# The second channel product of the last four groups, by seven block products instead of eight

## The chip, the cores and the metric

The kernel runs on one core of a Trainium2 chip. The core has five engines that each work through their own queue in order: TensorE (PE, matrix products into PSUM), VectorE (DVE) and ScalarE (ACT) for elementwise work, GpSimd (POOL) and SyncE (SP); DMA transfers are issued from the queues of SP, ACT and POOL. The metric is the device time of one execution in microseconds; lower is better.

## The reference, cut to what matters

The input is 2048 tokens of 512 channels. A state-space convolution along the tokens comes first, then a mixer block, each under layer norms and modulations. What matters here is the tail of the mixer:

```python
x1 = x + hs                                   # hs: shifted mixing product @ w2
h2 = _gelu(_layernorm(x1, axis=-1) @ w3) @ w4 # w3: 512 x 1376, w4: 1376 x 512
return x1 + h2
...
x = x + gb * _B_ref(h, B_w1, B_w2, B_w3, B_w4)
```

All is float32. The kernel multiplies in the reduced format fp32r and keeps the precision by splitting each operand into a high part (the value rounded to fp32r) and a low part (the rest): a product a·b is computed as ah·bh + ah·bl + al·bh, three matmuls in place of one.

## The kernel before

The first 360 us or so compute the convolution and the first mixing steps. The end, from `chan(0)` on, is eight groups of 256 tokens (two tiles of 128 tokens; block `b = 2g + i` of the residual `X2`). The order of instructions on every engine is written out by hand: inside the manual schedule each engine executes its instructions in program order.

A group has its 256 normalised tokens transposed in `hl` (high and low parts, four tiles of 128 channels each). Then, on TensorE:

- `first(f2)` (`chan_first`, L953): 256 columns of `w3` (two chunks of 128, `f = 2 f2` and `2 f2 + 1`), 24 matmuls that stream 256 tokens each, into one of two PSUM buffers `pm`. ScalarE evaluates gelu twice from that buffer, once rounded (`gh`) and once in float32 (`gf`); VectorE forms `gl = gf - gh` (L964). `f2 = 5` is only 96 columns.
- `second(f2)` (`chan_second`, L982 with L972, L973, L980): for both token tiles `i` the products of `gh` and `gl` with rows of `w4`, streaming 512 output columns each, summed over all 11 chunks in two PSUM banks `pa0`, `pa1`: 22 matmuls for each of the three lines in a group, 66 in all.
- the next group's part: `chan_w2` (L918), the mixing product `hs` of the next group, 24 matmuls of 512 columns into two PSUM buffers `ph`; the residual is added by VectorE (L916), then statistics (L779, L780; `rstd` on GpSimd, L774 and L775), `chan_norm` (L938), `chan_add` (L944, L945) and eight transposes (L812) whose high and low parts (`parts_of`, L815) are the next group's `hl`.

A group runs first(0), first(1), second(0), first(2), second(1), and so on, so that each `second` lies one `first` behind the `first` that feeds it. At its end `chan_out` (L988) multiplies both sums by the modulation `mods[5]`, adds them to `X2` (L991, L992) and issues the output DMAs (L995). Groups 1 to 3 also carry the first mixing product (`mix_half`, with `w1`) of a later group; groups 4 to 7 don't. Group 7 has no next group, and its last `second` calls are reordered so that the sums of tile 0 end before those of tile 1.

PSUM has eight banks, all in use here: two for transposes (`pT`), two `pm`, two `ph`, `pa0` and `pa1`.

Of the kernel before, what the change touches and what calls it, by code (L numbers as in the profile page):

```python
# [7 lines left out]
F32 = mybir.dt.float32  # L8
F32R = mybir.dt.float32r
# [104 lines left out]
def body(ctx, tc, A):  # L114
# [697 lines left out]
                    T.transpose(ps[j][:, k % 2, i * 128:i * 128 + 128], x[:, i, k * 128:k * 128 + 128], ident)  # L812
        return ps

    def parts_of(ps):  # L815
        hi = [cm.tile([128, 2, 256], F32R, name=f"nh{j}") for j in range(2)]
        lo = [cm.tile([128, 2, 256], F32R, name=f"nl{j}") for j in range(2)]
        for j in range(2):
            act(hi[j], ps[j])
            V.tensor_sub(lo[j], ps[j], hi[j].bitcast(F32))  # L820
        return [hi[k // 2][:, k % 2] for k in range(4)], [lo[k // 2][:, k % 2] for k in range(4)]
# [23 lines left out]
    def mix_norm(g):  # L845
        h, mv, r, nm = mh[g]
        for i in range(2):
            act(h[:, i], h[:, i], AF.Identity, scale=r[:, i:i + 1], bias=nm[:, i:i + 1])

    def three(p, wh, wl, hl, c):  # L850
        hi, lo = hl
        for k in range(4):
            T.matmul(p, wh[:, k, c], hi[k], start=(k == 0), stop=False)  # L853
            T.matmul(p, wl[:, k, c], hi[k], start=False, stop=False)  # L854
        for k in range(4):
            T.matmul(p, wh[:, k, c], lo[k], start=False, stop=(k == 3))  # L856
# [40 lines left out]
        V.tensor_sub(w, w.bitcast(F32), wh.bitcast(F32))  # L897
        win[g] = wh, w

    def chan_mod(g, i):  # L900
        if i == 0:
            cn[g] = cm.tile([128, 2, 512], F32, name="h2")
        modulate(cn[g][:, i], 2 * g + i)

    def chan_sum(g, i):
        wh, wl = win[g]
        p = psm.tile([128, 512], F32, name="ph")
        s = slice(i * 128, i * 128 + 128)
        for f in range(4):
            T.matmul(p, wh[:, f, s], W2h[:, f], start=(f == 0), stop=False)  # L910
            T.matmul(p, wh[:, f, s], W2l[:, f], start=False, stop=False)  # L911
        for f in range(4):
            T.matmul(p, wl[:, f, s], W2h[:, f], start=False, stop=(f == 3))  # L913
        if i == 1:
            del win[g]
        return lambda: V.tensor_add(cn[g][:, i], cn[g][:, i], p)  # L916
# [13 lines left out]
        rstd(r, mv[:, :, 1])  # L930
        cs[g] = mv, r

    def chan_norm(g):
        h = cn[g]
        mv, r = cs.pop(g)
        n = cm.tile([128, 2, 512], F32, name="h2")
        for i in range(2):
            V.tensor_scalar(n[:, i], h[:, i], mv[:, i, 0:1], r[:, i:i + 1], op0=OP.subtract, op1=OP.mult)  # L938
        return n
# [10 lines left out]
        act(go, p, AF.Gelu_apprx_tanh)  # L950
        mix_out(t, hf, go)

    def chan_first(hl, f2):  # L953
# [5 lines left out]
        gf = c2p.tile([128, 2, 256], F32, name="gf")  # L959
# [4 lines left out]
        V.tensor_sub(gl[:m, :ne], gf[:m, :ne], gh[:m, :ne].bitcast(F32))  # L964
        return gh, gl, ne, m

    def second_high(acc, part, f2, i):
        gh, gl, ne, m = part
        s = slice(i * 128, i * 128 + 128)
        for e in range(ne):  # L970
            f = f2 * 2 + e
            T.matmul(acc[i], gh[:m, e, s], W4h[:m, f], start=(f == 0), stop=False)  # L972
            T.matmul(acc[i], gh[:m, e, s], W4l[:m, f], start=False, stop=False)  # L973

    def second_low(acc, part, f2, i):
# [9 lines left out]
        for i in range(2):  # L985
            second_low(acc, part, f2, i)

    def chan_out(g, acc, i, qs):  # L988
        b = 2 * g + i
        o = c2p.tile([128, 512], F32, name="gf")  # L990
        V.tensor_mul(o, acc[i], mods[5])  # L991
        V.tensor_add(X2[:, b], X2[:, b], o)  # L992
        n = 128 // len(qs)
        for k, q in enumerate(qs):
            q.dma_start(A["out"][b, k * n:k * n + n], X2[k * n:k * n + n, b])  # L995

    def chan(g, hl):
        t = g + 3 if 0 < g < 4 else None
        nx = g + 1 if g < 7 else None
        acc = [psm.tile([128, 512], F32, name=f"pa{i}", bufs=1) for i in range(2)]  # L1000
        part, st = {}, {}

        def first(f2):
            part[f2] = chan_first(hl, f2)

        def second(f2):
            chan_second(acc, part.pop(f2), f2)

        def mod(i):
            if t is not None:  # L1010
                if i == 0:
                    mix_mod1(t)
                    mix_mod2(t, 0)
                else:
                    mix_mod2(t, 1)
                    mix_norm(t)

        def turn():
            if t is not None:
                st["hl"] = parts_of(transposed(mh.pop(t)[0]))  # L1020

        def half(hf):
            if t is not None:
                mix_half(t, st["hl"], hf)
                if t < 6:
                    first_stat(2 * t + 2 + hf)

        def nxt(f, *a):
            if nx is not None:
                return f(nx, *a)  # L1030

        if g == 0:
            first(0)
# [25 lines left out]
        else:  # L1059
            first(0)  # L1060
            mod(0)
            first(1)
            mod(1)
            second(0)
            nxt(chan_split)
            first(2)
            nxt(chan_mod, 0)
            second(1)
            turn()
            nxt(chan_mod, 1)  # L1070
            first(3)
            half(0)
            second(2)
            nxt(chan_w2)
            nxt(chan_stats)
            first(4)
            n = nxt(chan_norm)
            nxt(chan_add)
            half(1)
            second(3)  # L1080
            first(5)
            r = parts_of(transposed(n)) if nx is not None else None
            if g < 7:
                second(4)
            if g < 6:
                chan_load(g + 2)
            if g < 7:
                second(5)
            else:
                second_high(acc, part[4], 4, 0)  # L1090
                second_high(acc, part[4], 4, 1)
                for i in range(2):
                    second_low(acc, part[4], 4, i)
                    second_high(acc, part[5], 5, i)
                    second_low(acc, part[5], 5, i)
        for i in range(2):
            chan_out(g, acc, i, (Y,) if g < 7 else (Y, S))
        return r

    splits = []  # L1100

# [13 lines left out]
    with tc.manual_schedule():  # L1115
# [190 lines left out]
        first_stats(4)  # L1306
        chan_load(1)
        for g in range(8):
            r = chan(g, r)


# [16 lines left out]
```

## Time and profile before

| what | value |
|---|---|
| time, median of 3 runs | 678.95 us (677.28 to 679.72) |
| time of the profiled execution | 677.66 us |
| its span, first to last instruction | 675.9 us |
| mean granted TensorE clock | 0.997 |
| TensorE busy, share of the span | 94% |
| VectorE, ScalarE, GpSimd busy | 73%, 50%, 17% |
| group 3 | 487.50 to 530.72 us, 43.22 us |
| groups 4, 5, 6 | 36.56 us each, from 530.72 us to 640.40 us |
| group 7 | from 640.40 us, last matmul at about 670.6 us |

Rows of the profile name an engine, a source line, the tile written and the tiles read, the shape, a count, and times in microseconds (means in ns). PE is the matmul, PEld the loading of the stationary operand ahead of it. The chain of waits lists the work that ended last, in order of time: a start, the time counted for it, and the instruction. A matmul is recorded with its whole latency, so neighbours overlap; in the chain each is counted only with what it adds.

### The profile page before, as it was taken

The numbers are of one execution on the slowest core, as the hardware profiler recorded it, in microseconds if no ns is written. First come the engines' busy times: TensorE is split into PE (matmuls) and PEld (weight loads), VectorE is DVE, ScalarE is ACT, GpSimd is POOL, SyncE is SP. The second block draws the span as 40 slices with busy tenths as digits, with TensorE's granted clock in tenths as the row PEclk, the third lists the DMA queues.
The fourth block names the chain that finished last, engine by engine and source line by source line (L and its number), as shares of the span: only waits on it lengthen the run. The fifth ranks groups of instructions, "written<-read, shape, count | busy, mean of one in ns | idle before, by whom it ended". The sixth has DMA issues, their size and how long they took to land.

```text
span 675.9 us, 16884 instructions
## 1 busy us (share of the span) xinstructions
PE 636.7 (94%) x7205; PEld 508.2 (75%) x7205; DVE 494.2 (73%) x797; ACT 335.8 (50%) x511; POOL 113.7 (17%) x220
## 2 busy tenths in 40 slices
PE   2899999999999998988999999999999999999996
PEld 1556555665568876645889899898998989898895
DVE  7889999999996897897889777454674445363622
ACT  5778998898884666624456334132141213122121
POOL 2102212112207133203643002010010000000000
PEclk9999999999999999998999999999999999999999
DMA  9602274642838999966386020110100201010001
GB/s 318 277 2 75 75 230 107 197 136 76 294 71 296 302 361 377 366 199 194 118 267 232 1 64 1 55 40 16 57 22 31 64 18 46 1 63 1 1 32 31
DMA packets 49923, 86.43 MB, mean 128 GB/s; under 512 B 4532, under 2 KB 38328, under 8 KB 47256
## 3 DMA queue, kind: packets, MB, share of 16 engines
q1 hardware_dynamic: 44904, 60.97, 28.3%
q0 software_dynamic: 4624, 23.86, 9.8%
q8 instruction: 56, 0.92, 0.6%
q10 hardware_dynamic: 320, 0.52, 0.3%
q14 instruction: 19, 0.16, 0.1%
HBM read 59.12 MB, written 32.90 MB: 136 GB/s over the span
## 4 chain that ended last, share of the span: by engine, by line
PE 72%; DMA 5%; DVE 5%; ACT 3%; issue 2%; POOL 1%; SPq 1%; ACTq 0%; DVEq 0%; POOLq 0%
PE xx L440 7%; PE pm L856 7%; PE pm L854 7%; PE pm L853 7%; PE pa L972 6%; PE pa L973 6%; PE pa L980 6%; PE pk L673 4%; PE kp L490 3%; DMA w4l<-Dw 2%; PE pz L695 2%; PE pk L643 2%; PE ph L911 2%; PE ph L910 2%; PE ph L913 2%
## 5 line engine op out<-in xcount | busy, mean ns | idle before, releaser
L122 ACT ACTIVATE gh<-pm 128x512 fp32r<-128x512 f32 (+1 forms) x48 | 26.9, 561 | 199.2 <-PE pm L856 199.2
L853 PE MATMUL pm<-nh,w3h 128*128 128x256 f32 (+1 forms) x352 | 85.9, 278 | 0.0
L854 PE MATMUL pm<-nh,w3l 128*128 128x256 f32 (+1 forms) x352 | 85.7, 279 | 0.1
L964 DVE TENSOR_TENSOR gl<-gf,gh 128x512 fp32r<-128x512 f32 (+1 forms) x48 | 30.9, 643 | 68.1 <-ACT gf L122 68.1
L972 PE MATMUL pa<-w4h,gh 128*128 128x512 f32 (+1 forms) x176 | 69.6, 395 | 0.0
L973 PE MATMUL pa<-w4l,gh 128*128 128x512 f32 (+1 forms) x176 | 68.9, 392 | 0.0
L854 PEld LDWEIGHTS pm<-nh,w3l 128*128 128x128 f32 (+1 forms) x352 | 65.2, 185 | 2.0 <-DVE w3l L767 0.3
L853 PEld LDWEIGHTS pm<-nh,w3h 128*128 128x128 f32 (+1 forms) x352 | 65.3, 186 | 1.4
L856 PE MATMUL pm<-nl,w3h 128*128 128x256 f32 (+1 forms) x352 | 54.9, 277 | 0.1
L774 POOL TENSOR_TENSOR rs<-mv,eps_t 128x1 f32<-128x1 f32 (+1 forms) x35 | 9.2, 264 | 267.3 <-DVE mv L780 251.5
L980 PE MATMUL pa<-w4h,gl 128*128 128x512 f32 (+1 forms) x176 | 48.0, 390 | 0.0
L441 PE MATMUL xx<-MG,ON 64*128 64x512 f32 x160 | 47.1, 390 | 0.0
L440 PE MATMUL xx<-MG,ON 64*128 64x512 f32 x160 | 47.1, 390 | 0.0
L856 PEld LDWEIGHTS pm<-nl,w3h 128*128 128x128 f32 (+1 forms) x352 | 46.6, 185 | 0.3 <-DVE nl L820 0.3
L916 DVE TENSOR_TENSOR h<-h,ph 128x512 f32<-128x512 f32 x16 | 11.0, 688 | 45.0 <-PE ph L913 45.0
L458 DVE SCALAR_TENSOR_TENSOR e<-tr,p 128x512 f32<-128x512 f32 x64 | 41.1, 684 | 1.7 <-ACT tr L122 1.4
L467 DVE TENSOR_TENSOR e<-tr,p 128x1024 f32<-128x1024 f32 x32 | 39.0, 1218 | 1.1 <-ACT tr L122 1.1
L490 PEld LDWEIGHTS kp<-e,e 128*32 128x32 f32 x2048 | 30.1, 110 | 12.7 <-issue 7.5
L468 DVE TENSOR_TENSOR e<-tr,m 128x1024 f32<-128x1024 f32 x32 | 39.0, 1218 | 0.0
L122 ACT ACTIVATE p<-xx 128x1024 f32<-128x1024 f32 (+1 forms) x40 | 37.5, 980 | 2.1 <-PE xx L258 0.6
L980 PEld LDWEIGHTS pa<-w4h,gl 128*128 128x128 f32 (+1 forms) x176 | 33.0, 188 | 7.1
L673 PE MATMUL pk<-VK,xu 64*64 64x128 f32 x768 | 35.9, 270 | 2.2 <-issue 2.2
(259 smaller groups left out, 1709.8 us busy)
## 6 DMA issues: line engine op xcount, KB each, us to landing
VU<-vs SPq DMA_DIRECT2D x64, 128.0 KB, 3.6
ld<-VU SPq DMA_DIRECT2D x16, 512.0 KB, 7.5
ZT<-z POOLq DMA_DIRECT2D x30, 256.0 KB, 6.3
Dw<-in_w POOLq DMA_DIRECT2D x8, 688.0 KB, 4.6
xu<-in_u SPq DMA_DIRECT2D x4, 1024.0 KB, 8.6
KX<-in_x POOLq DMA_DIRECT2D x4, 1024.0 KB, 9.0
ld<-ZT SPq DMA_DIRECT2D x8, 512.0 KB, 5.6
win<-GD SPq DMA_DIRECT2D x32, 128.0 KB, 2.5
```

What stands on the lines that cost most here:

```text
L122: return S.activation(out, in_, f, bias=bias, scale=scale)
L440: T.matmul(x[:, :512], la, ma, start=(i == 0), stop=(i == len(ops) - 1))
L441: T.matmul(x[:, 512:], lb, mb, start=(i == 0), stop=(i == len(ops) - 1))
L458: V.scalar_tensor_tensor(e0[:, 1, a], tr[:, 1, 0], 1.0 - 2.0 * a, mg[:, a], op0=OP.mult, op1=OP.mult)
L490: T.matmul(kp[32 * j:32 * j + 32, (k % 2) * 4 + g], e1[:, r, d], e0[:, r, :, d * 32:d * 32 + 32], start=(r == 0), stop=(r == 1), skip_grou ...
L673: T.matmul(p[gh][kk * 64:kk * 64 + 64, i, ro], w, VK[jh][rows, ri * 32 + k1].rearrange("p j g -> p (j g)"), start=(ri == 0), stop=(ri == 1 ...
L853: T.matmul(p, wh[:, k, c], hi[k], start=(k == 0), stop=False)
L854: T.matmul(p, wl[:, k, c], hi[k], start=False, stop=False)
L856: T.matmul(p, wh[:, k, c], lo[k], start=False, stop=(k == 3))
L972: T.matmul(acc[i], gh[:m, e, s], W4h[:m, f], start=(f == 0), stop=False)
L973: T.matmul(acc[i], gh[:m, e, s], W4l[:m, f], start=False, stop=False)
L980: T.matmul(acc[i], gl[:m, e, s], W4h[:m, f], start=False, stop=(f == 10))
```

## The change

For groups 4 to 7 `chan` is replaced by `chan_late`. There, two neighbouring chunks of the hidden columns (a pair `p`, chunks 2p and 2p+1), the two token tiles and the two halves of the 512 output columns are taken as a 2 x 2 by 2 x 2 block product, and computed with seven block products (Winograd's form of Strassen's scheme) instead of eight. A block product is 128 x 128 x 256.

- `pair_load`, `pair_sums`, `pair_split`: for each of five pairs, four blocks of `w4` (128 x 256) are loaded by DMA into rows of `X2` that are no longer needed, combined in place by four subtractions on VectorE, and split into high parts (ScalarE) and low parts (VectorE). Pairs 0 to 2 are made in group 3, pairs 3 and 4 in group 4. They live where `W1h`, `W1l`, spare tiles and unused halves of `W4h`, `W4l` are.
- `fast_first` replaces `chan_first` for five pairs (four in group 7): gelu once over 512 columns to `xa` and once over 384 to `ha`; four sums of 128 columns on VectorE (`xs`), their high part `hs` on ScalarE, then the low parts `la` (384) and `ls` (512) on VectorE.
- `fast_second` replaces `chan_second` for a pair: 21 matmuls that stream 256 columns, into eight half banks `R[0]` to `R[7]` (`pa0`, `pa1` and both `ph`).
- `fast_rest`: chunk 10 (96 rows), 12 matmuls of 256 columns.
- `fast_sum` replaces `chan_out`: VectorE combines the eight half banks (a copy and six sums of 256, one of 512), and then multiplies and adds to `X2` as before. In group 7 it comes between first(4) and first(5), with a copy and five sums, and chunks 8 to 10 go the old way into the transposes' banks.
- `chan_w2_late`: the next group's mixing product uses the `pm` buffers, since both `ph` are taken.

```diff
+    def pair_sums(p):
+        x = praw[p]
+        V.tensor_sub(x[0], x[1], x[0])
+        V.tensor_sub(x[1], x[3], x[1])
+        V.tensor_sub(x[3], x[3], x[0])
+        V.tensor_sub(x[2], x[2], x[3])
...
+    def fast_first(hl, f2):
...
+        act(fl(xa), pf, AF.Gelu_apprx_tanh)
+        act(fl(ha)[:, 128:], pf[:, 128:], AF.Gelu_apprx_tanh)
+        V.tensor_add(xs[:, 0], xa[:, 0], xa[:, 2])
+        V.tensor_sub(xs[:, 2], xa[:, 1], xa[:, 0])
+        V.tensor_sub(xs[:, 1], xs[:, 0], xa[:, 1])
+        V.tensor_sub(xs[:, 3], xa[:, 3], xs[:, 1])
+        act(hs, xs)
+        V.tensor_sub(fl(la)[:, 128:], fl(xa)[:, 128:], fl(ha)[:, 128:].bitcast(F32))
+        V.tensor_sub(ls, xs, hs.bitcast(F32))
...
+    def fast_second(R, part, p):
...
+        turns = ((0, ha[:, 1], la[:, 1], bh["11"], bl["11"]), (1, ha[:, 3], la[:, 3], bh["21"], bl["21"]),
+                 (4, ha[:, 2], la[:, 2], th[2], tl[2]), (5, hs[:, 3], ls[:, 3], bh["22"], bl["22"]),
+                 (2, hs[:, 2], ls[:, 2], th[1], tl[1]), (3, hs[:, 0], ls[:, 0], th[0], tl[0]),
+                 (6, hs[:, 1], ls[:, 1], th[3], tl[3]))
+        for r, x, _, wh, wl in turns:
+            T.matmul(R[r], x, wh, start=(p == 0 and r in (0, 4, 2, 6)), stop=False, skip_group_check=True)
+            T.matmul(R[r], x, wl, start=False, stop=False, skip_group_check=True)
+        for r, _, x, wh, wl in turns:
+            T.matmul(R[r], x, wh, start=False, stop=False, skip_group_check=True)
...
+    def fast_sum(g, banks, R, rest=True):
+        o = row2(4)
+        q = o.rearrange("p i (h c) -> p (i h) c", h=2)
...
+        V.tensor_copy(q[:, 1], R[0])
+        V.tensor_add(q[:, 2], q[:, 1], R[1])
+        V.tensor_add(q[:, 1], q[:, 1], R[6])
+        for j in range(2):
+            V.tensor_add(q[:, 3 * j], q[:, 1], R[2 + j])
+        V.tensor_add(q[:, 1], q[:, 0], R[3])
+        if rest:
+            V.tensor_add(q[:, 1], q[:, 1], R[7])
+        V.tensor_add(q[:, 0::3], q[:, 0::3], v(banks[2]))
+        for i in range(2):
+            b = 2 * g + i
+            V.tensor_mul(o[:, i], o[:, i], mods[5])
+            V.tensor_add(X2[:, b], X2[:, b], o[:, i])
...
     def chan(g, hl):
...
+            if g == 3:
+                pair_sums(0)
             half(1)
             second(3)
+            if g == 3:
+                pair_split(0, blocks(W1h)[:4], blocks(W1h)[4:])
+                pair_sums(1)
+                pair_sums(2)
             first(5)
...
+            if g == 3:
+                pair_split(1, blocks(W1l)[:4], blocks(W1l)[4:])
+            second(4)
+            chan_load(g + 2)
+            if g == 3:
...
+                pair_split(2, blocks(t4[0]) + blocks(t4[1]), blocks(t4[2]) + blocks(t4[3]))
+                pair_load(3, 4)
+            second(5)
...
+    def chan_late(g, hl):
...
+        first(0)
+        if g == 4:
+            pair_load(4, 6)
+            pair_sums(3)
+            pair_split(3, *[[w[:, 2 * n, 256:512] for n in range(4)] for w in (W4h, W4l)])
+        first(1)
+        second(0)
+        nxt(chan_split)
+        first(2)
+        if g == 4:
+            pair_sums(4)
+            pair_split(4, *[blocks(cm.tile([128, 2, 512], F32R, name="h2")) for _ in range(2)])
+        second(1)
+        nxt(chan_mod, 0, row2(6))
+        first(3)
+        nxt(chan_mod, 1)
+        second(2)
+        if g == 7:
+            second(3)
+            first(4)
+            fast_sum(g, banks, R, False)
+            first(5)
...
+            second_high(acc, part[4], 4, 0, 8)
+            second_high(acc, part[4], 4, 1, 8)
+            for i in range(2):
+                second_low(acc, part[4], 4, i)
+                second_high(acc, part[5], 5, i)
+                second_low(acc, part[5], 5, i)
+            for i in range(2):
+                chan_out(g, acc, i, (Y, S), X2[:, 6 + i])
+            return
+        chan_w2_late(nx)
+        chan_stats(nx)
+        first(4)
+        n = chan_norm(nx, row2(4))
+        chan_add(nx)
+        second(3)
+        first(5)
+        parts_of(transposed(n), hl)
+        second(4)
+        if g < 6:
+            chan_load(g + 2)
+        fast_rest(R, part[5])
+        fast_sum(g, banks, R)
+        return hl
...
-            r = chan(g, r)
+            r = chan(g, r) if g < 4 else chan_late(g, r)
```

More of the change, by code (lines that the diff above doesn't have):

```diff
@@ L971, in second_high @@
             f = f2 * 2 + e
-            T.matmul(acc[i], gh[:m, e, s], W4h[:m, f], start=(f == 0), stop=False)
+            T.matmul(acc[i], gh[:m, e, s], W4h[:m, f], start=(f == f0), stop=False)
             T.matmul(acc[i], gh[:m, e, s], W4l[:m, f], start=False, stop=False)
@@ L986, in chan_second, with row2, blocks, pair_load @@
             second_low(acc, part, f2, i)
-    def chan_out(g, acc, i, qs):
+    def row2(b):
+        return X2[:, b:b + 2]
+    def blocks(t, n=2):
+        f = t.rearrange("p a b -> p (a b)")
+        return [f[:, 256 * i:256 * i + 256] for i in range(f.shape[1] // 256)]
+    praw, pslot = {}, {}
+    def pair_load(p, b):
+        praw[p] = blocks(row2(b))
+        for n in range(4):
+            r = (2 * p + n // 2) * 128
+            Y.dma_start(praw[p][n], WD["w4"][r:r + 128, n % 2 * 256:n % 2 * 256 + 256])
@@ new lines, in pair_sums, with pair_split @@
+    def pair_sums(p):
[4 more added lines that the diff above has]
+        V.tensor_sub(x[2], x[2], x[3])
+    def pair_split(p, hi, lo):
+        pslot[p] = hi, lo
+        x = praw.pop(p)
+        for n in range(4):
+            act(hi[n], x[n])
+        for n in range(4):
+            V.tensor_sub(lo[n], x[n], hi[n].bitcast(F32))
+    four = lambda t: t.rearrange("p a (c b) -> p (a c) b", c=2)
+    fl = lambda t: t.rearrange("p a b -> p (a b)")
@@ new lines, in fast_rest @@
+    def fast_rest(R, part):
+        gh, gl, ne, m = part
+        for x, ws in ((gh, (W4h, W4l)), (gl, (W4h,))):
+            for r, i, h in ((1, 1, 0), (5, 1, 1), (4, 0, 0), (7, 0, 1)):
+                for w in ws:
+                    T.matmul(R[r], x[:m, 0, i * 128:i * 128 + 128], w[:m, 10, h * 256:h * 256 + 256],
+                             start=False, stop=(x is gl), skip_group_check=True)
+    def fast_sum(g, banks, R, rest=True):
+        o = row2(4)
+        q = o.rearrange("p i (h c) -> p (i h) c", h=2)
+        v = lambda t: t.rearrange("p (h c) -> p h c", h=2)
+        V.tensor_copy(q[:, 1], R[0])
[11 more added lines that the diff above has]
+            V.tensor_add(X2[:, b], X2[:, b], o[:, i])
+            if rest:
+                Y.dma_start(A["out"][b], X2[:, b])
@@ L1063, in chan @@
             mod(1)
+            if g == 3:
+                for p in range(3):
+                    pair_load(p, 2 * p)
             second(0)
-            nxt(chan_split)
+            chan_split(nx)
             first(2)
-            nxt(chan_mod, 0)
+            chan_mod(nx, 0)
             second(1)
             turn()
-            nxt(chan_mod, 1)
+            chan_mod(nx, 1)
             first(3)
@@ L1081, in chan @@
             first(5)
[L1082 to L1088, printed above, removed]
-            else:
[L1090 to L1095, printed above, removed]
```

115 lines of the change are left out of this document (75 added, 40 removed).

## The prediction

> **What bounds the kernel now.** I read the page first, then the busy times by stage, then the chain of waits. The stages shown are groups 4, 5 and 7 (6 is as 5); columns are the stage, its length, then busy time and count by engine.
>
> ```profile
> span 675.9 us, 16884 instructions
> ```
>
> ```profile
> core 0: us, PE busy (x) PEld busy (x) DVE busy (x) ACT busy (x) POOL busy (x), PEclk, DMA share, GB/s
> ...
> 530.72:567.28 36.56, 36.56 (x232) 32.89 (x232) 18.15 (x30) 8.01 (x15) 0.89 (x2) 1.00 0.09 29
> 567.28:603.84 36.56, 36.56 (x232) 32.88 (x232) 18.15 (x30) 8.01 (x15) 0.89 (x2) 1.00 0.09 30
> 640.40:670.40 30.00, 30.00 (x198) 27.16 (x197) 7.25 (x12) 6.09 (x12) 0.00 (x0) 1.00 0.05 18
> ```
>
> In groups 4 to 7 TensorE has no gap at all: every matmul taken out is time won, as long as nothing else makes it wait. VectorE is half idle (18.15 of 36.56 us), yet it works in program order, so what counts is when a particular result is due, not its share.
>
> The chain gives the pace of matmuls: start, time counted, instruction.
>
> ```profile
> 551.72 0.91 PE ph L913 x4
> 554.44 0.91 PE ph L913 x4
> 559.92 0.91 PE pa L980 x4
> 561.77 0.48 PE pm L856 x4
> 562.25 0.87 PE pT L812 x8
> 569.57 0.45 PE pm L856 x4
> 570.93 0.45 PE pm L856 x4
> ```
>
> ```profile
> L856 PEld LDWEIGHTS pm<-nl,w3h 128*128 128x128 f32 (+1 forms) x352 | 46.6, 185 | 0.3 <-DVE nl L820 0.3
> ```
>
> From 551.72 to 554.44 lie 12 matmuls of 512 columns: 2.72/12 = 0.227 us each. From 569.57 to 570.93 lie 12 of 256: 1.36/12 = 0.113, exactly half. So shorter matmuls keep the column rate, with a stationary load for each, whose 0.185 runs ahead of the matmuls. A `first` (24 of 256) is 2.72 us, first(5) 561.77 + 0.48 − 560.83 = 1.42, the transposes 0.87.
>
> **What the change removes on TensorE.** A group's second product was 66 × 0.227 = 14.96 us. It becomes 5 × 21 + 12 = 117 matmuls of 256 columns, 13.26 us: 1.70 less for groups 4, 5, 6. In group 7 four pairs go fast (84 of 256) and 18 of 512 remain: 9.52 + 4.08 = 13.60, so 1.36 less. Together **6.46 us**. The new pieces: a fast second is 21 × 0.113 = 2.38, the rest 1.36.
>
> **What it adds on VectorE and ScalarE.** Rows by form, then VectorE's end of a group in order of time:
>
> ```profile
> L964 DVE TENSOR_TENSOR gl<-gf,gh 128x512 fp32r<-128x512 f32 x40 | 27.5, 688 | 59.7 <-ACT gf L122 59.7
> L897 DVE TENSOR_TENSOR win<-win,wh 128x1024 fp32r<-128x1024 f32 x8 | 9.8, 1226 | 12.3 <-ACT wh L122 10.2 <-DMA w4l<-Dw 2.0
> L938 DVE TENSOR_SCALAR h<-h,mv,rs 128x512 f32<-128x512 f32 x14 | 7.0, 542 | 0.0
> L265 DVE TENSOR_TENSOR p<-p,WN 128x256 f32<-128x256 f32 x8 | 3.3, 419 | 0.0
> L537 DVE TENSOR_TENSOR KX<-DS,KX 128x64 f32<-128x64 f32 x1 | 0.3, 274 | 0.0
> ```
>
> ```profile
> 603.65 0.69 DVE L991 TENSOR_TENSOR gf<-pa,modg 128x512 f32<-128x512 f32 x1 [2.05 <-PE pa L980]
> 604.37 0.69 DVE L992 TENSOR_TENSOR KX<-KX,gf 128x512 f32<-128x512 f32 x1
> 604.98 0.68 DVE L991 TENSOR_TENSOR gf<-pa,modg 128x512 f32<-128x512 f32 x1
> 605.70 0.69 DVE L992 TENSOR_TENSOR KX<-KX,gf 128x512 f32<-128x512 f32 x1
> ```
>
> ```profile
> L122 ACT ACTIVATE gh<-pm 128x512 fp32r<-128x512 f32 x40 | 23.9, 597 | 174.7 <-PE pm L856 174.7
> L122 ACT ACTIVATE wh<-win 128x1024 fp32r<-128x1024 f32 x8 | 8.4, 1055 | 0.0
> L122 ACT ACTIVATE w4h<-w4l 128x512 fp32r<-128x512 f32 x10 | 5.8, 631 | 0.0
> L122 ACT ACTIVATE w3h<-w3l 128x352 fp32r<-128x352 f32 x4 | 1.7, 496 | 0.0
> ```
>
> An operation that needs the one before starts 0.72 us after it (603.65 to 604.37: 0.03 beyond its length), one that doesn't 0.61 (0.08 short of it). So 256 columns cost 0.34 to 0.45. A sum of 128 columns has no row; it lies between the 0.274 of 64 and the 0.419 of 256. I take 0.32 by the line between them.
>
> - `fast_sum`: copy and six sums of 256, mostly in a chain, 2.9; one of 512, 0.7; the old four of 512 as above, 2.74. **6.3 us** (bounds 7 × 0.34 + 5 × 0.61 = 5.4 and 7 × 0.45 + 5 × 0.72 = 6.8) where `chan_out` took 2.74.
> - `fast_first`: four sums of 128 with two dependent steps, **1.15** (0.9 to 1.4); then `hs` on ScalarE, 512 from SBUF as the row of `w4h`, **0.63**; `la` 0.55, `ls` 0.69. Before, VectorE had one operation of 0.69.
> - `pair_sums` and low parts: five times eight operations of 256, 1.6 + 1.4 = 3.0 us a pair; on ScalarE four copies of about 0.4 (below the 0.496 of 352 columns), which lie in its idle time (it is busy 8.01 of 36.56 us) except where said; bare, they would be 1.6 a pair. The 20 loads of 128 KB on SP are issued a group ahead, and behind them wait only loads for the next group.
>
> Now where each is due. t = 0 is an edge of the stage windows.
>
> **Start of groups 5, 6, 7.** When a buffer `pm` is ready shows in ScalarE's start:
>
> ```profile
> 606.62 0.60 ACT L122 ACTIVATE gh<-pm 128x512 fp32r<-128x512 f32 x1 [6.15 <-PE pm L856]
> 609.40 0.60 ACT L122 ACTIVATE gh<-pm 128x512 fp32r<-128x512 f32 x1 [1.69 <-PE pm L856]
> ```
>
> Against 603.84, first(0) is ready at 2.78 and first(1) at 5.56. TensorE then has six matmuls of second(0) that need only `ha`; the seventh, on `hs`, would start near 6.0. But `fast_sum` of the group before stands ahead on VectorE: 0 to 6.3, four sums to 7.45, `hs` to 8.15. Stall **2.2 us** (bounds: 5.4 + 0.9 + 0.6 = 6.9, so 0.9; 6.8 + 1.4 + 0.7 = 8.9, so 2.9). Afterwards each `fast_first` has a `first` and a `second` (5.1 us) to spare against a chain of 0.6 + 1.15 + 0.63 + 0.69, and keeps up. Near the end the transposes wait for `chan_norm`, now behind first(4)'s longer chain: 0.66 + 1.15 + 0.66 + 0.72 + 0.95 (two of 0.54) = 4.1 against second(3) + first(5) = 3.8, of which the second half of the norm alone is late: **0.2** (0 to 0.6). Groups 5 and 6: −1.70 + 2.4 = +0.7 each.
>
> **Group 3.** Ahead of first(5)'s `gl` VectorE gets three `pair_sums` and one low split, 3 × 1.6 + 1.4 = 6.2.
>
> ```profile
> 523.40 0.69 DVE L945 TENSOR_TENSOR KX<-KX,h 128x512 f32<-128x512 f32 x1
> 526.41 0.42 DVE L964 TENSOR_TENSOR gl<-gf,gh 96x256 fp32r<-96x256 f32 x1 [2.32 <-ACT gf L122]
> 526.90 1.29 DVE L820 TENSOR_TENSOR nl<-pT,nh 128x512 fp32r<-128x512 f32 x2
> ```
>
> ```profile
> 530.10 0.62 PE L980 MATMUL pa<-w4h,gl 96*128 96x512 f32 x2
> ```
>
> From 524.0 they run to 530.2, `gl` to 530.6, its matmuls were due at 530.10: stall **0.5** (0 to 1.5). The next `nl` (1.3) still comes in time, but two low splits push `chan_out` to 534.7 to 537.4.
>
> **Group 4** starts at 531.2. VectorE: `chan_out` to 6.2, sums to 7.3, `hs` 8.0: stall **2.0**. Then pair 3's sums and split (to 11.6), with ScalarE's copies ahead of first(1)'s gelu: `hs` of first(1) at 13.4 against 13.1, **0.3**. `chan_split` (1.06 and 1.23) to 15.6, `fast_first` to 18.1, pair 4 to 21.1, two modulations and `fast_first` of first(3) to 26.5, so the residual add that frees the `pm` bank of `chan_w2_late` ends at 27.2, where first(4) was due at 25.65: **1.55**. That wait is new: the bank was `ph`, which nothing else wanted. The norm 0.2. Sum 4.05 (1.5 to 7); net +2.35.
>
> **End of group 7.** `fast_sum` stands between the `gl` of first(4) and that of first(5). Rows of the same places now:
>
> ```profile
> 661.87 0.45 PE pm L856 x4
> ...
> 666.00 0.47 PE pm L856 x4
> ```
>
> ```profile
> 662.36 0.60 ACT L122 ACTIVATE gh<-pm 128x512 fp32r<-128x512 f32 x1 [4.40 <-PE pm L856]
> 663.48 0.69 DVE L964 TENSOR_TENSOR gl<-gf,gh 128x512 fp32r<-128x512 f32 x1 [4.79 <-ACT gf L122]
> ```
>
> From first(4)'s end (662.32): `gl` to 1.85; copy, five sums, one of 512, four of 512: 5.85, to 7.6; `gl` of first(5) 8.0. TensorE has first(5) 1.42, eight high matmuls 1.81, and two and two 0.91: the matmul that needs it is due at 4.0. Stall **4.0** (3.2 to 4.5). Everything after it (1.4 us of matmuls, multiply, add, output DMA) moves along. Group 7: −1.36 + 2.2 + 4.0 = +4.85.
>
> **Sum:** 0.5 + 2.35 + 0.7 + 0.7 + 4.85 = +9.1 us. The profiled execution took 677.66 (span 675.9 and 1.76 around it), which gives 686.8; over the median of the runs, 678.95, it gives 688.05. I forecast **687.5**.
>
> One more thing speaks against a gap of 4 us. Earlier in this trace TensorE waited once for 3.7 us, and the granted clock fell behind it:
>
> ```profile
> PE py L723 <- DMA ld<-ZT: 3.7, 1, 3.7
> ```
>
> ```profile
> 304.00:308.00 4.00, 2.19 (x32) 1.09 (x32) 0.52 (x2) 0.60 (x1) 0.00 (x0) 0.86 1.00 323
> 308.00:312.00 4.00, 3.31 (x38) 1.49 (x35) 3.52 (x8) 1.45 (x3) 1.80 (x4) 0.71 0.72 237
> ```
>
> At half pace the 1.4 us of matmuls behind the gap would cost another 1.4; I leave it out of the sum and in the upper bound, since the gap is only just that long. [...]
>
> **Rivals.**
>
> - *VectorE hides it all, faster.* If small operations follow each other at their slope alone ((0.688 − 0.419)/256 = 1.05 ns a column: 0.27 for 256, 0.54 for 512), `fast_sum` is 4.6, the start of a group has no stall, and the end of group 7 keeps about 1.9, group 4 about 1: 677.66 − 6.46 + 2.9 = 674.1. The starts stall by `fast_sum` less 4.2 each, the tail by `fast_sum` less 2.2, the rest by some 2.5, so it decides from a `fast_sum` under 4.7. For it: VectorE is half idle. Against: 0.61 between independent operations above. Chance 0.10.
> - *Stalls at their low ends, nothing to see.* 0 + 1.5 + 0.9 + 0.9 + 0.9 + 3.2 = 7.4 less 6.46: 678.6 to 682. Chance 0.14.
> - *Worse.* If second(0) of group 4 waits until the split into the upper halves of `W4h` and `W4l` has ended (11.6 in place of 8.0), +3.6, with the half clock 1.4: 692, up to 696 with the high bounds. For it: the same tiles are written and read there. Against: the halves don't overlap. Chance 0.12.
> - *The matmuls aren't cheaper.* Were a 256-column matmul bound by its load, 0.185 us, the 117 would cost 8.4 more a group: beyond 700. The pace of 0.113 with a load each is against it. Chance 0.02.
>
> **Numbers.** Forecast 0.62, with its own range 682.5 to 692. What can be told from no change is 0.5%, 675.6 to 682.3. Faster 0.10, same 0.14, slower 0.62 + 0.12 + 0.02 = 0.76. The range 679 to 694 leaves out the faster rival and the worst end, about 0.18.
>
> **What would show it.** Right: TensorE idle about 2 us behind the second `first` of groups 4 to 7 with ScalarE's `hs` as releaser, 1.5 in group 4 ahead of first(4) for VectorE's residual add, 4 us at the end for the last `gl`; groups 5 and 6 about 37.3 us long. Wrong: groups of 34.9 us, or these gaps absent with `fast_sum` well under 5 us; or a pace other than 0.113 in `fast_second`.

## The result, and the profile after

The changed kernel takes 689.81 us (median of 4 runs, 689.51 to 690.66); the kernel before, run beside it on the same chip, takes 678.26 us. The ratio is **1.0171**, 95% interval 1.0147 to 1.0194: 1.7% slower, clear of the noise. The forecast was 687.5 us in a range of 679 to 694. One execution each of e3_nosums, e5_pool, e7_order and e8_moving ran far longer than the others (807 to 2162 us); the times given are medians of all executions, and the ratios leave those four out.

The head of the page after, and its busy times. The span grew by 11.8 us, and VectorE's busy time by 56.7 us:

```profile
span 687.7 us, 17525 instructions
...
PE 638.4 (93%) x7394; PEld 516.0 (75%) x7394; DVE 550.9 (80%) x967; ACT 352.6 (51%) x550; POOL 113.6 (17%) x220
```

TensorE's waits from group 3 to the end, after (engine, tile and line, releaser: us in total, times, longest). Before, this view is empty for the same stretch:

```profile
PE ph L1057 <- ACT gf L122: 5.6, 4, 1.5
PE pT L984 <- DVE gl L968: 4.2, 1, 4.2
PE pa L984 <- DVE gl L968: 0.7, 1, 0.7
PE pm L856 <- DVE KX L919: 0.7, 1, 0.7
```

L1057 is the high matmul of `fast_second`; `gf` is the tile that holds `hs`. So the first row is the wait behind the second `first` of groups 4 to 7, the second the tail of group 7, the third group 3, the fourth the new wait of group 4 for the residual add (L919) that frees a `pm` bank.

The stages after: groups 4, 5, 6, 7 and the last four microseconds, with the columns of the stages before (length, busy time and count by engine, granted clock, DMA):

```profile
531.40:569.35 37.95, 36.11 (x280) 34.21 (x279) 33.88 (x79) 13.52 (x28) 0.89 (x2) 1.00 0.18 57
569.35:607.08 37.73, 36.21 (x283) 34.72 (x283) 28.69 (x62) 10.64 (x20) 0.88 (x2) 1.00 0.09 29
607.08:644.78 37.70, 36.18 (x283) 34.69 (x283) 28.69 (x62) 10.65 (x20) 0.88 (x2) 1.00 0.04 15
644.78:682.42 37.64, 31.93 (x239) 29.78 (x237) 22.65 (x51) 8.08 (x16) 0.00 (x0) 0.93 0.04 15
679.00:683.00 4.00, 2.93 (x6) 1.82 (x6) 2.36 (x5) 0.00 (x0) 0.00 (x0) 0.50 0.02 6
```

Groups 4, 5 and 6 are 1.4, 1.2 and 1.1 us longer in these windows than the 36.56 of before, and group 7 is 37.6 where it took 30.2. (The window of group 4 ends 0.4 us short: from its `first(0)` to the next it is 38.35 us, 1.8 more than before.) In the last four microseconds the granted clock is 0.50.

The chain of waits at the start of group 6, after (start, time counted, instruction). It leaves TensorE, walks through `fast_sum` on VectorE, the four sums of `fast_first`, `hs` on ScalarE, and comes back to TensorE 8.27 us after the edge at 607.08:

```profile
607.23 0.44 DVE KX L1075
...
613.01 0.69 DVE KX L1087
613.71 0.20 DVE KX L1038
...
614.35 0.30 DVE KX L1041
...
614.67 0.64 ACT gf L122
...
615.35 0.39 PE ph L1057
```

The chain of the same kernel at the tail of group 7. `gl` of first(4) (672.34), then `fast_sum` (673.04 to 679.09), then `gl` of first(5), and only then TensorE; its last matmuls of 512 columns count 0.43 each, where they counted 0.227:

```profile
672.34 0.69 DVE gl L968
673.04 0.35 DVE KX L1075
...
678.40 0.69 DVE KX L1087
679.09 0.34 DVE gl L968
...
679.48 1.65 PE pT L984 x3
...
681.55 0.43 PE pT L977
```

The pace away from the waits, from the chain of the same kernel, a `first` and the `fast_second` behind it:

```profile
617.39 0.12 PE pm L856
...
618.34 0.47 PE pm L859 x4
...
620.24 0.12 PE pa L1057
...
622.74 0.12 PE pm L856
```

The 24 matmuls of the `first` take 620.24 − 617.39 = 2.85 us, 0.119 each, and the 21 of the `fast_second` 2.50, also 0.119. The forecast had 0.113 for both.

### The profile page after: what moved, and what is told of

It reads as the page before. It is cut to its first block, busy times and chain, and to the rows that moved or that the text cites. A ratio compares the mean times of both kernels' runs of the same rounds, so it can differ in the third digit from the quotient of the medians.

```text
span 687.7 us, 17525 instructions
## 1 busy us (share of the span) xinstructions
PE 638.4 (93%) x7394; PEld 516.0 (75%) x7394; DVE 550.9 (80%) x967; ACT 352.6 (51%) x550; POOL 113.6 (17%) x220
## 4 chain that ended last, share of the span: by engine, by line
PE 64%; DVE 12%; DMA 4%; ACT 3%; issue 3%; POOL 1%; SPq 0%; ACTq 0%; DVEq 0%; POOLq 0%
PE xx L440 7%; PE pm L859 5%; PE pm L856 5%; PE pm L857 5%; PE pk L673 4%; PE kp L490 3%; PE pa L976 3%; PE pa L977 3%; PE pa L984 3%; PE pz L695 2%; DMA w4l<-Dw 2%; PE pk L619 2%; PE pk L643 2%; PE pu L418 2%; PE xx L258 1%
## 5 line engine op out<-in xcount | busy, mean ns | idle before, releaser
L122 ACT ACTIVATE gh<-pm 128x512 fp32r<-128x512 f32 (+2 forms) x48 | 24.7, 515 | 96.1 <-PE pm L859 96.1
L122 ACT ACTIVATE KX<-pm 128x512 f32<-128x512 f32 (+1 forms) x26 | 14.5, 559 | 60.4 <-PE pm L859 56.1
L673 PEld LDWEIGHTS pk<-VK,xu 64*64 64x64 f32 x768 | 33.2, 133 | 5.8 <-issue 5.0
L122 ACT ACTIVATE tr<-xx,hpi 128x1024 f32<-128x1024 f32 x32 | 35.8, 1118 | 2.9 <-PE xx L441 1.5
L122 ACT ACTIVATE tr<-xx 128x1024 f32<-128x1024 f32 x32 | 33.0, 1030 | 8.3 <-PE xx L441 6.9
L490 PE MATMUL kp<-e,e 128*32 128x64 f32 x2048 | 35.2, 221 | 0.3 <-DVE e L468 0.3
L976 PE MATMUL pa<-w4h,gh 128*128 128x512 f32 (+1 forms) x88 | 34.9, 396 | 0.0
```

The source lines that it names most:

```text
L122: return S.activation(out, in_, f, bias=bias, scale=scale)
L490: T.matmul(kp[32 * j:32 * j + 32, (k % 2) * 4 + g], e1[:, r, d], e0[:, r, :, d * 32:d * 32 + 32], start=(r == 0), stop=(r == 1), skip_grou ...
L673: T.matmul(p[gh][kk * 64:kk * 64 + 64, i, ro], w, VK[jh][rows, ri * 32 + k1].rearrange("p j g -> p (j g)"), start=(ri == 0), stop=(ri == 1 ...
L976: T.matmul(acc[i], gh[:m, e, s], W4h[:m, f], start=(f == f0), stop=False)
```

## The experiments

All comparisons are against the kernel before on the same chip. The way to the first transpose of group 3 varies by some 5 us between the profiled executions (524.2 us in e7_order, 529.1 in e1_tail), so beside the time I give one distance inside the trace: from the first transpose of group 3 to the end of the last matmul. It is 145.1 us before and 157.1 after.

| kernel | time, us | ratio (95%) | group 3 transposes to end, us |
|---|---|---|---|
| before | 678.26 | | 145.1 |
| after | 689.81 | 1.0171 (1.0147 to 1.0194) | 157.1 |
| e1_tail | 686.03 | 1.0123 (1.0086 to 1.0161) | 151.8 |
| e2_defer | 684.94 | 1.0100 (1.0071 to 1.0130) | 151.7 |
| e3_nosums | 675.05 | 0.9956 (0.9939 to 0.9974) | 141.7 |
| e5_pool | 697.14 | 1.0281 (1.0244 to 1.0318) | |
| e6_all | 685.01 | 1.0105 (1.0070 to 1.0140) | 151.7 |
| e4_halves | 681.79 | 1.0055 (1.0030 to 1.0080) | 147.7 |
| e8_moving | 680.78 | 1.0032 (1.0011 to 1.0053) | 147.7 |
| e9_rows | 680.85 | 1.0042 (1.0017 to 1.0067) | 147.7 |
| e10_place | 680.94 | 1.0028 (1.0012 to 1.0045) | 147.1 |
| e7_order | 677.05 | 0.9967 (0.9953 to 0.9980) | 142.8 |
| e11_both | 676.08 | 0.9953 (0.9933 to 0.9973) | 142.5 |

### The tail alone: fast_sum ahead of first(4) in group 7

```diff
-            first(4)
             fast_sum(g, banks, R, False)
+            first(4)
             first(5)
```

> The changed kernel with one move: in group 7 fast_sum stands ahead of first(4) in place of behind it. If VectorE's order makes the gap of 4.36 us at the end and the gap makes the halved clock (1.3 us), both go: fast_sum then runs 0.2 to 6.1 us after second(3), gl of first(4) ends at about 6.7, and TensorE needs it at 5.9, so a gap of some 0.7 is left: 689.8 - 4.36 - 1.3 + 0.7 = 684.8 us, and a granted clock of 1.00 to the end. Rival, the gap belongs to the last products themselves (their operands or banks): 689.8, within 1.

The distance fell by 5.3 us. The waits of this kernel:

```profile
PE ph L1057 <- ACT gf L122: 6.1, 4, 1.6
...
PE pT L984 <- DVE gl L968: 0.2, 1, 0.2
```

The wait at the tail went from 4.2 to 0.2, and the granted clock over the last two microseconds is 1.00. So of the 5.3 us the wait itself was 4.0, and the other 1.3 were the half clock that followed it. The median time fell by 3.8 us only, but the four executions spread over 4.0 us (684.21 to 688.22).

### The starts alone: the last part of fast_sum behind the next group's fast_first(0)

The multiplications by `mods[5]`, the residual adds and the output DMAs (L1084 to L1089) become a function that the next group calls behind its `fast_first(0)`.

```diff
+        def finish():
+            for i in range(2):
+                b = 2 * g + i
+                V.tensor_mul(o[:, i], o[:, i], mods[5])
+                V.tensor_add(X2[:, b], X2[:, b], o[:, i])
...
+        if rest:
+            owed.append(finish)
...
+        if owed:
+            owed.pop()()
```

> The changed kernel with one move: the last part of fast_sum (two multiplications, two additions, the output DMA; 2.74 us of VectorE) is done behind fast_first(0) of the next group in place of ahead of it. If VectorE's order makes the gap at the start of groups 5, 6, 7 (1.77 us each), it goes: hs would be written 2.7 us earlier, before it is due. 689.8 - 5.3 = 684.5 us; 686 to 687 if part of it turns up again at the second pair. Group 4 keeps its gap of 1.4. Rival, second(0) waits for the half banks that fast_sum reads: unchanged, 689.8, within 1.

The distance fell by 5.35 us. The row of the start waits:

```profile
PE ph L1057 <- ACT gf L122: 1.1, 1, 1.1
```

Of the four start waits only that of group 4 is left, which follows the old `chan_out` of group 3. Three waits of 1.5 us by the records were worth 5.35/3 = 1.78 each. The place of 2.74 us of VectorE's work in the order was the cause of them: with that work moved and nothing else changed, they are gone.

### The new sums left out

```diff
-        V.tensor_add(xs[:, 0], xa[:, 0], xa[:, 2])
-        V.tensor_sub(xs[:, 2], xa[:, 1], xa[:, 0])
-        V.tensor_sub(xs[:, 1], xs[:, 0], xa[:, 1])
-        V.tensor_sub(xs[:, 3], xa[:, 3], xs[:, 1])
-        act(hs, xs)
...
-        V.tensor_sub(ls, xs, hs.bitcast(F32))
-        return ha, la, hs, ls
+        return ha, la, ha, la
```

The products that used the sums read `ha` and `la` instead, and the order of e1_tail is kept.

> The matmuls of the changed kernel without what feeds the sums: the four sums of activations, their high part on ScalarE and their low part on VectorE are left out in all of fast_first, and the products that used them take ha and la; fast_sum stands ahead of first(4) in group 7 as in e1_tail. The gaps at the starts and in group 4 go; group 3 keeps its 0.9. What is left is the saving of 6.46 and the pace. If the slower pace (0.118 in place of 0.113 a matmul of 256 columns, 0.9 us a group) belongs to the short matmuls and their number of waits, 678.3 - 6.46 + 3.4 + 0.9 = 676.2 us. If it comes from VectorE's and ScalarE's traffic in SBUF, which is less here, the pace goes back to 0.113 to 0.115: 673 us.

Without the sums of activations there is no wait left but those for `gl` (0.7 us in group 3, 0.3 at the end). A stretch of one group's length in this kernel, from a point of group 5 to the same point of group 6 (the others are as long):

```profile
569.84:605.10 35.26, 35.26 (x283) 34.30 (x283) 20.75 (x38) 7.47 (x15) 0.89 (x2) 1.00 0.10 31
```

TensorE has no gap here, and yet a group takes 35.26 us where 36.56 − 1.70 = 34.86 were forecast for a group without stalls. The missing 0.4 us are the pace of the matmuls, and nothing of it is a wait. The matmuls of a `first` were at 0.113 again for the most part, those of `fast_second` near 0.118. At 675.05 us it lies between the two cases that were expected: the pace came back in part. So with the new sums of activations free, and at the pace that its operands happen to have, the change would be 0.44% below before.

### The weight blocks' sums on GpSimd

```diff
-        V.tensor_sub(x[0], x[1], x[0])
+        P.tensor_tensor(x[0], x[1], x[0], op=OP.subtract)
...
-            V.tensor_sub(lo[n], x[n], hi[n].bitcast(F32))
+            P.tensor_tensor(lo[n], x[n], hi[n].bitcast(F32), op=OP.subtract)
```

e5_pool is the changed kernel with this edit, e6_all has it together with the edits of e1_tail and e2_defer.

> The changed kernel with the twenty sums and twenty low parts of the weight blocks on GpSimd in place of VectorE. If these operations are what makes VectorE late in groups 3 and 4, group 3's gap of 0.98 us ahead of the last products goes, chan_out is no longer late, so group 4's gap at its second(0) is gone or under 0.3 (1.42 before), and the residual add that frees the bank comes in time (0.94): 689.8 - 3.3 = 686.5 us. Rival, GpSimd is slower on blocks of 256 columns than the groups allow, and second(3) or second(4) of group 4 waits for the blocks: a gap of some us there, 689 us or more.

> The three moves together: fast_sum ahead of first(4) in group 7, its last part behind fast_first(0) of the next group, the weight blocks on GpSimd. If the gaps are separate costs they add: 689.8 - 5.3 - 5.3 - 3.3 = 675.9 us, just faster than before (678.3). Rival, VectorE is then short elsewhere and gaps come back: 678 to 681.

The gain came in neither; e6_all is above its rival as well. The loss of e6_all is in group 4 alone, which takes 44.9 us from one `first(0)` to the next, where groups 5 and 6 take 35.8. The GpSimd groups (line, engine, operation, tiles, shape, count, busy us, mean ns, idle before) and TensorE's wait:

```profile
L1021 POOL TENSOR_TENSOR w1h<-KX,w1h 128x256 fp32r<-128x256 f32 x4 | 4.6, 1184 | 0.0
...
L1021 POOL TENSOR_TENSOR w1l<-KX,w1l 128x256 fp32r<-128x256 f32 x4 | 2.8, 743 | 0.0
```

```profile
PE ph L1057 <- ACT gf L122: 4.4, 2, 3.2
```

GpSimd takes 0.74 to 1.18 us by these groups for a subtraction of 256 columns that costs VectorE 0.42. The wait in group 3 is gone, but TensorE now waits 4.4 us at the start of group 4, 3.2 of them in one piece, and behind that piece TensorE ran at half clock:

```profile
538.00:542.00 4.00, 0.81 (x5) 0.64 (x4) 3.96 (x6) 0.63 (x1) 3.24 (x5) 0.77 0.29 86
542.00:546.00 4.00, 4.00 (x20) 4.00 (x20) 0.25 (x1) 0.84 (x2) 2.78 (x4) 0.50 0.65 217
```

VectorE's first two sums of activations in that stretch:

```profile
537.66 0.80 DVE L1038 TENSOR_TENSOR KX<-KX 128x128 f32<-128x128 f32 x1 [3.54 <-POOL w1l L1021]
538.38 0.81 DVE L1039 TENSOR_TENSOR KX<-KX 128x128 f32<-128x128 f32 x1
```

Two things hold VectorE up. The sums write a row of `X2` in which the blocks of pair 1 still lie, and GpSimd forms the low part of that pair from them (`w1l`) until 538.32: the first sum waits for it by the profile, and the second starts when it has ended. And the four sums take 0.70 to 0.81 us each, where the same lines take 0.28 to 0.29 in the changed kernel, with GpSimd at work beside them (busy for 3.24 of the 4.00 us from 538 to 542). Whether GpSimd's work makes them longer isn't shown: no run here separates it from other causes. e5_pool lost some 7 us against the changed kernel; where it lost them isn't shown.

### All the order at once, on VectorE

e7_order has the edits of e1_tail and e2_defer, and two more moves: in group 3 the three `pair_sums` go ahead of `chan_w2`, and in group 4 the sums and split of pair 4 go between the two residual adds of `chan_w2_late` (and, since the blocks of pair 4 now stay longer in their rows of `X2`, two other results of group 4 change rows).

```diff
+            if g == 3:
+                for p in range(3):
+                    pair_sums(p)
             nxt(chan_w2)
...
+            if pair and i == 0:
+                pair_sums(4)
+            elif pair:
+                pair_split(4, *[blocks(cm.tile([128, 2, 512], F32R, name="h2")) for _ in range(2)])
```

> The changed kernel with four orders changed and no work left out: fast_sum of group 7 ahead of first(4); the last part of each fast_sum (multiply and residual add) behind the next group's fast_first(0); in group 3 the three pair_sums ahead of chan_w2; in group 4 the sums and split of pair 4 between the two residual adds of chan_w2_late. Everything stays on VectorE. Theory (each stall of the changed kernel is VectorE's order, not its amount): 689.8 less 5.3 for the tail, less 5.3 for the starts (both as measured one at a time), less 1.0 for the stall in group 3, less some 2.4 of the stalls in group 4: 675.8, with the only stall over 0.5 us left in group 4. Rival (VectorE has too little room in group 4, the stall only moves): 678 to 681, with a wait for KX or gl in group 4 in its place.

677.05 us, ratio 0.9967 (0.9953 to 0.9980): **0.3% faster than before**, with the whole of the computation. By the distance from group 3 it is 14.3 us below the changed kernel, and the expectation's four terms were 14.0. Of the waits from group 3 to the end one is left, 0.2 us for the last `gl`. VectorE does the same work (551.1 us busy against 550.9), so the stalls that this view lists were order, not amount. A stretch of one group's length, from the transposes of group 4 to those of group 5 (the next is as long):

```profile
559.99:595.77 35.78, 35.76 (x283) 34.48 (x282) 28.60 (x63) 10.64 (x20) 0.88 (x2) 1.00 0.10 31
```

35.78 us a group is 0.78 below before, less than half of the 1.70 that the count of matmuls promised. Of the 0.92 that is missing, 0.30 is the wait of the transposes for the norm, which these four moves leave (1.09 us from the first transpose to the next matmul, 0.79 before). The other 0.6 is what the next runs are about.

### The pace of 256-column matmuls

e4_halves is the kernel before, with each matmul of `second` in groups 4 to 7 cut into two of 256 columns. Nothing else is changed, so at 0.113 each it would take the same time.

```diff
-            T.matmul(acc[i], gh[:m, e, s], W4h[:m, f], start=(f == 0), stop=False)
+            for c in halves():
+                T.matmul(acc[i][:, c], gh[:m, e, s], W4h[:m, f, c], start=(f == 0 and c.start in (None, 0)), stop=False, skip_group_check=True)
```

> The kernel before with one edit: in groups 4 to 7 each matmul of the second product is cut into two of 256 columns into the halves of its bank; no block products, no sums, the same waits. If matmuls of 256 keep the pace of 0.113 (my prediction's step), nothing changes: 678.3, within 1. If a group without matmuls of 512 runs at 0.118 as the changed kernel does, 264 matmuls a group at 0.0045 more, some 0.9 to 1.2 us a group: 682 to 683 us.

A group took 37.22 us, 0.66 more, with TensorE busy without a gap. The chain shows where: a `first` at 0.113 and a `second` at 0.12 with nothing waited for in either.

```profile
586.12 0.11 PE pm L853
...
587.48 0.12 PE pa L978
...
589.38 0.96 PE pa L987 x8
590.34 0.23 PE ph L910
```

From 587.48 to 590.34 lie 24 matmuls: 0.119 each. From 586.12 to 587.48 lie 12: 0.113. So the pace isn't a property of 256 columns, and it is lost in the new shape of `second` even without the sums. Three edits of this kernel look for the cause. e8_moving issues neighbours that share the moving operand:

```diff
+                for c in halves():
+                    for w in (W4h, W4l):
+                        for i in range(2):
+                            mm(i, gh, e, w, c, w is W4h)
```

> The kernel before with its second product of groups 4 to 7 in halves of 256 columns as in e4_halves (681.8), in another order (group 7's last two calls as there): two matmuls in a row stream the same half row of w4 with different stationary operands, as first does with its tokens. If the pace of 0.118 to 0.120 comes from a new moving operand with every matmul, it goes back to 0.113: 678.3 to 679. If not: 681 to 682.

e9_rows issues all that goes into one half bank of PSUM in a row:

```diff
+            for c in halves():
+                for i in range(2):
+                    for e in range(ne):
+                        mm(i, gh, e, W4h, c, True)
+                        mm(i, gh, e, W4l, c)
```

> As e8_moving, in a third order: six matmuls in a row into the same half bank in place of two, nearer to first's twelve. If the slower pace comes from going back and forth between PSUM regions, it goes back towards 0.113: 678.5 to 679.5. If not: 681 to 682.

Neither moved it: 37.21 us a group in both. The order of operands and the alternation of PSUM banks are not the cause. e10_place moves the pool of the stationary operands:

```diff
-        c2p = ctx.enter_context(tp("c2p", 2))
+        c2p = ctx.enter_context(tp("c2p", 2, side="right"))
```

> The kernel before with the second of groups 4 to 7 in halves of 256 columns (as in e4_halves, which took 681.8 and 0.119 us a matmul), and the pool of gh, gl and gf allocated from the other end of SBUF, away from w4. If the pace hangs on where the two operands lie: 0.113 us a matmul in the second, groups of 36.6 us, 678.3 to 679. If it doesn't: groups of 37.2 us, 680.5 to 682.

By its time it falls into the second case (680.94 us, groups of 37.10). But the chain shows something neither case had:

```profile
613.50 0.91 PE pa L987 x8
...
615.36 0.47 PE pm L856 x4
...
617.25 0.12 PE pa L978
...
619.14 0.94 PE pa L987 x8
```

Eight matmuls of a `second` now run at 0.91/8 = 0.113, which never happened in e4_halves. The same line in the next `second`, with the other buffer of `gl` and the next rows of `w4`, runs at 0.118, and a `first`, mostly at 0.113 in e4_halves, runs at 0.118 between them. Groups 5 and 6 show the same pattern: second(0) and second(3) near 0.113, second(1) and second(2) near 0.118. In the allocation the pool had moved by only 1216 bytes of each partition, since the allocations from both ends nearly meet. So the place matters, though the move didn't win the time. e11_both puts the same edit on e7_order:

> e7_order with the pool of the stationary operands (gh, gl, gf and those of fast_first) allocated from the other end of SBUF. If place sets the pace, 0.9 us a group less than e7_order, groups 5 and 6 near 34.9 us: about 672.5. If not, the same time as e7_order within 0.5.

Groups of 35.8 us as in e7_order, and 676.08 us with an interval (0.9933 to 0.9973) that overlaps with that of e7_order: this placement gains nothing that can be told.

e12_bench measures the disputed cost by itself. Behind the last product of the kernel before stand 39 blocks of 24 matmuls, each on its own line, with operands at fixed places; their sums aren't used.

```diff
+            q = psw.tile([128, 2, 256], F32, name="pm")[:, 0]
+            ends = [(n == 0, n == 23) for n in range(24)]
+            [T.matmul(q, W3h[:, 0, 0:128], hl[0][0], start=a, stop=z) for a, z in ends]
+            [T.matmul(q, hl[0][0][:, 0:128], W4h[:, 0, 0:256], start=a, stop=z) for a, z in ends]
...
+            [T.matmul(q, hl[0][0][:, 0:128], W4h[:, 0, 32:288], start=a, stop=z) for a, z in ends]
...
+            [T.matmul(q, part[4][0][:, 0, 0:128], W4h[:, 0, 0:256], start=a, stop=z) for a, z in ends]
```

> The kernel before, with 39 blocks of 24 matmuls of 256 columns behind its last product (their sums are read by nobody; the work of the kernel itself is unchanged), each block on a line of its own with one stationary and one moving operand at fixed places, TensorE alone: those of a first; the normalised tokens or gh against ten chunks of w4h or w4l, by halves, and at offsets of 32, 64 and 128 columns; w3h against w4h; both from w4h. Some 680 + 39 x 24 x 0.113 to 0.120 = 786 to 792 us. Theory (the pace is set by where the two operands lie against each other): blocks that differ only in the place of the moving operand fall into two kinds, 0.113 and 0.118 to 0.120, with a pattern over the chunks. Rival 1 (the pace is set by the traffic of other engines): all blocks at 0.113. Rival 2 (by the pair of tensors, w4 as such, not by places): all blocks with w4 alike at 0.120, and those of a first at 0.113.

784.29 us in one run, a little under the 786 to 792 expected, with the kernel before at 678.15. The chain counts each block as a piece; L1102 to L1121 are the normalised tokens against ten chunks of `w4h` by halves, L1122 to L1124 the same at offsets of 32, 64 and 128 columns, L1125 on `gh` against `w4h` and then `w4l`, L1135 and L1136 both operands from `w4h`, L1137 both from the tokens' tile, L1138 `w3h` against `w4h`, L1139 `w3h` against the tokens as in a `first`:

```profile
675.61 2.72 PE pm L1102 x24
...
730.01 2.83 PE pm L1122 x24
...
735.66 2.83 PE pm L1124 x24
738.49 2.88 PE pm L1125 x24
...
770.17 2.88 PE pm L1136 x24
773.05 2.88 PE pm L1137 x24
775.92 2.87 PE pm L1138 x24
778.80 2.74 PE pm L1139 x24
```

```profile
675.44:729.84 54.40, 54.40 (x482) 54.40 (x481) 0.00 (x0) 0.00 (x0) 0.00 (x0) 1.00 0.02 6
738.33:767.13 28.80, 28.80 (x243) 28.80 (x242) 0.00 (x0) 0.00 (x0) 0.00 (x0) 1.00 0.00 1
```

All twenty blocks of L1102 to L1121 run at 54.40/480 = 0.1133, all ten with `gh` at 28.80/240 = 0.1200, with VectorE, ScalarE and GpSimd idle and the clock at 1.00. Rival 1 (traffic of other engines) can't be the cause of these. Rival 2 (the tensor `w4` as such) falls too: the same `w4h` as moving operand runs at 0.113 against the tokens' tile and at 0.120 against `gh` or `w3h`. The pace changed only where the pair of operands did, so the pair of places is what is left of the three. No pattern over the chunks of one tensor showed, contrary to the theory's words. But the blocks of one pace stand next to each other and their order wasn't varied, so a pace that is handed on from one block to the next isn't excluded, for the three at offsets above all.

That a pace can be handed on shows in e7_order. From group 4 on the tokens of the next group are written into the same tiles, so first(0) and first(1) of groups 6 and 7 have the same operands in the same places:

```profile
601.94 0.45 PE pm L859 x4
...
637.77 0.47 PE pm L859 x4
```

In group 6 their 48 matmuls take 5.47 us (601.01 to 606.48), 0.114 each; in group 7 they take 5.60 (636.82 to 642.42), with the first 30 or so at 0.118 and the rest at 0.113. So the places of a matmul's operands alone don't set its pace.

## Why the prediction was right, and the step of it that failed

**The direction and the mechanism: right.** The waits stand where they were forecast, with the releasers that were named: `hs` behind the second `first` of groups 4 to 7, the residual add in group 4 ahead of first(4), the last `gl` at the end, `gl` of first(5) in group 3. e1_tail, e2_defer and e7_order show that they hang on VectorE's program order.

Term by term, in us:

| term of the sum | forecast | measured | from |
|---|---|---|---|
| less work on TensorE, four groups | −6.46 | about −3.4 | e7_order against before, the waits that are left taken out |
| group 3, `gl` behind the pair sums | 0.5 | 0.7 (1.0 by the length of the group) | wait on `pa` |
| group 4, start | 2.0 | 1.1 | wait left in e2_defer |
| group 4, `hs` of first(1) | 0.3 | none | waits |
| group 4, bank of `chan_w2_late` | 1.55 | 0.7 (2.5 with the start, by the length) | wait on `pm`; 38.35 against 35.87 of e7_order |
| groups 5, 6, 7, start | 2.2 each | 1.78 each | e2_defer |
| groups 4 to 6, norm before the transposes | 0.2 each | 0.3 each | starts of the matmuls, 1.09 against 0.79 |
| tail of group 7 | 4.0 | 4.2 | wait on `pT` |
| half clock behind the tail | not in the sum | 1.3 | e1_tail |

**The step that failed is "exactly half. So shorter matmuls keep the column rate".** The forecast took 0.113 for each 256-column matmul of `fast_second` from twelve matmuls of one `first`. After the change the pace is 0.118 to 0.120, in `fast_second` and in many of the `first`s around it, and nearly half of the saving was never there: 0.6 us in each of groups 4 to 6 and 1.1 in group 7, 3.0 in all. Why the pace is slower stays open. The contrary rows were in the prediction's own fences: the four matmuls of first(5) that count 0.48, and first(5) as a whole, 1.42 for twelve, are 0.118 to 0.120 each, and the 0.47 at 666.00 is 0.118 each. I used the 1.42 as the length of first(5) and didn't see that it contradicts the 0.113. The rival "matmuls aren't cheaper" was drawn at 0.185, the load's own duration, far beyond what happened; a bound from the row at hand, 0.118, would have put 0.6 us a group into the sum.

**The half clock was left out of the sum and came.** Before, behind the wait of 3.7 us, the granted clock was 0.50 from 307.0 to 310.2 us. After, it was 0.50 behind the 4.2 us wait of the tail as well: it fell inside the gap, 1.8 us behind the end of the last matmul ahead of it (675.29; granted 1.00 up to 677.0, 0.50 from 677.2 on). Shorter waits had it behind them too: 3.3 us, up to 304.87, in the changed kernel (0.50 from 306 to 308), and 3.2 us in e6_all by the records (3.36 between the starts of the matmuls around it, beyond one matmul). The one wait near 4 us in the trace at hand had the half clock behind it, and the gap was forecast at 4.0, so its 1.4 us belonged in the sum: 687.5 + 1.4 = 688.9, where 689.81 was measured.

**The stalls were over-estimated where the due time was set by TensorE.** The chain of the vector work itself was sized well: `fast_sum` takes 613.71 − 607.23 = 6.5 us (6.3 forecast), the four sums 0.94 (1.15), `hs` 0.64 (0.63), and `hs` ends 8.2 us behind the edge (8.15). What was off is its place against the matmuls. The forecast let `fast_sum` begin at the edge, 0.16 us behind the first matmul of the group (603.68 and 603.84 before), though its own row has VectorE begin at 603.65; after the change it begins 0.16 ahead of that matmul (607.23 and 607.39). And at the slower pace the 54 matmuls ahead of the seventh of second(0) take 6.3 us rather than 6.1. The two took back some 0.5 us at each start. In group 4 the residual add came sooner than reckoned, and the wait of 0.3 for the second `hs` did not arise.

**The sum came out near by errors of both signs, so the closeness is in part luck.** From one `first(0)` to the next the change cost 1.0 us in group 3 (44.22 against 43.24; 0.5 forecast), 1.8 in group 4 (2.35), 1.2 in groups 5 and 6 (0.7 each) and 6.9 in group 7 (4.85): 12.0 us against 9.1. The 3.0 of saving that is missing and the 1.3 of half clock stand against some 1.4 us of stalls that were smaller.

**What it says of the rival "VectorE hides it all".** As the change stands, it fell. But e7_order shows that VectorE has the room: with four moves in its order all but 0.2 us of the listed waits is gone, and the kernel lands 0.3% below before. It misses the 674.1 of that rival for the most part by the pace.

## What to carry to other kernels

When work moves from TensorE to a half idle engine, find for each result the moment at which it is due and what stands ahead of it in that engine's order: here all the loss of stalls (14 us with the half clock) and its cure lay in the order, with VectorE's amount of work unchanged. Take the price of an operation from all rows of its shape, not from the fastest stretch: the same 256-column matmul costs 0.113 or 0.120 us, and nearly half of the saving was lost in that difference. Moving operations to a slower engine (GpSimd, 0.74 to 1.18 us against 0.42) made a wait of 3.2 us where reordering left 0.2 in all.

## What the runs showed of the hardware that was not expected

- The pace of back-to-back 256-column fp32r matmuls, each with its own stationary load, is 0.1133 us for some pairs of operand places and 0.1200 for others, with all other engines idle and the clock at 1.00 (e12_bench). No run here has these matmuls without their loads, so none shows whether the load has a part in the slower pace.
- What sets it is open. In the allocation of e12_bench, `w3h`, `w4h`, `w4l` and `gh` begin at bytes 23968, 68000, 90528 and 117152 of each partition, all 416 beyond a multiple of 512, and the tokens' tile at 163680, 352 beyond one. Every block near 0.120 has two operands with equal remainders, and every block near 0.113 has different ones. But that is no rule: L1124 has the remainders of L1102 and took 0.118, and in e10_place, where `gh` and `gl` begin 96 beyond a multiple of 512, every matmul of `second` has different remainders and most of them took 0.118.
- The pace isn't a matter of the operands' places alone: the same 48 matmuls on the same tiles took 5.47 us in group 6 and 5.60 in group 7 of e7_order.
- The granted clock fell to 0.50 behind idle stretches of 4.2 us (after) and 3.2 us (e6_all), 1.8 and 2.0 us after TensorE's last matmul.
- GpSimd took 0.74 to 1.18 us for subtractions of one shape, 128 x 256 in float32, within one stage of e6_all.
